# A planner's cost model recalibrated, and the stores of first contents held until the chunks of x are loaded

## The chip, the cores and the metric

One core of one Trainium2 chip. The metric is device time in microseconds (us) of one launch. The kernel before takes 1199.34 us, the median of 3 runs (1198.03 to 1200.96).

## The reference

Three layers follow one another on 2304 tokens (4 sequences of 576) of width 512.

```python
# attention with decay, 4 x 8 heads, 576 tokens, 64 wide
scores = q @ k.T / 8 + cum[:, None] - cum[None, :]      # cum: running sum of log f; causal
x = softmax(scores) @ v                                 # -> [2304, 512]
# dense MLP
h = x @ w_in                                            # [2304, 2048]
x = (h * sigmoid(1.702 * h)) @ w_out                    # [2304, 512]
# 8 experts, the best 2 for each token, noisy gate
logits = x @ w_gate + log1p(exp(x @ w_noise)) * noise
out[t] = sum over the 2 experts e: weight * (relu(x[t] @ w1[e]) @ w2[e])
```

## The kernel before, in words

**Precision.** Each operand of a product is split into a rounded part (`h`, hi) and the rest (`l`, lo), and a product is three matmuls: hi·hi, hi·lo, lo·hi. The rounding is done by `rounded` (lines 327 to 335), the rest by `subtract` (lines 337 and following). Both offer several ways: the rounding on VectorE (DVE, L333), ScalarE (ACT, L334) or GpSimd (POOL, L335), the subtraction on VectorE (L338) or GpSimd (L339). Both read and write SBUF alone.

**Stages.** The *attention* runs over 16 pairs of heads, four to a sequence (batch): loads of q, k and v, splits, scores (L600 to L666), maximum (DVE), exponential (ACT L589), transposes (L727), product with v (L773), store of the result to `x2` in DRAM (L781). The *dense MLP* runs over 9 chunks of 256 tokens and four quarters Q of its hidden width; a chunk in a quarter is 48 matmuls of 256 columns (`h`, L982) and 24 of 512 columns (`y`, L1002), with a gelu between (`gelu`, L957 to L961: tanh on ACT, a product on DVE, the split gh and gl). `xprep` (L920 and following) brings a chunk of x: four loads of 256 KB (L933: `xa` and a second summand into the tile that later is the hi part), two loads of the softmax's reciprocals (L938, into the later lo part), an addition and a multiplication (L927 on DVE or L928 on POOL), the rounding on ACT (L948) and the subtraction. Chunks 0 to 5 (`early_c`) do quarter 0 as *fillers* between the attention's products; their results go to DRAM (`yp`, L1050) and are read back later (`yload`, L1128, into `yacc`). The last two of them stay in SBUF (`kept`); chunks 0 to 3 (`back`) are loaded a second time. After the attention, quarter 0 runs over chunks 6, 7 and 8 (`rest`), and quarters 1 to 3 over kept, rest, back. The last quarter goes with *routing*: each chunk's rows are scattered into a table `tab` in DRAM (L1282). The *experts* then read the table, 640 slots each, and add their rows to `out` by scattering DMAs (L1524). Before that the table and `out` must hold their first contents: `prefill` stores 40 blocks of 258 KB to `tab` (L1076) and 23 blocks of 256 KB of zeros to `out` (L1079), all from one SBUF tile `padr`. It begins when the attention's end is planned (`a_done`) and has the lowest rank among that stage's transfers, 10200.

**The order of the work.** Nothing is ordered by hand. `Planner` runs every part as a thread of a modelled core while the program is built, and the instructions are written out in the order of the modelled start times; each engine then executes its queue in that order, so an instruction that waits holds up all behind it on its engine. A thread yields (engine, us, emit) or several such ways; the way that the model can start first is taken, and among those that can start at about the same time the lowest rank. Costs come from small formulas: `mm` for matmuls, `act`, `dve`, `pool1`, `pool2` for the vector engines, `dma` for transfers. A transfer holds SP's queue for 0.475 us, lands by the running total `moved`, and none is begun while `moved` is more than 2.1 us ahead (`DEEP`).

```python
self.moved = max(self.moved, t + 1.1) + us                 # run(): a transfer of `us`
us = max(self.moved, t + 0.475 * (starts - 1) + 1.1 + us / starts) - t
def mm(n, count=1):  return count * (max(n, MMN) / 2400 + 0.0025)      # MMN = 128
def dma(nbytes):     return 0.05 + nbytes / 360e3
yield ("DMA", 2.9, load, 4)                                # xprep: 1 MB of a chunk
yield ("go", one_op(("DMA", 1.46, rload, 2), rok))         # xprep: 512 KB of reciprocals
```

Of the kernel before, what the change touches and what calls it, by code (L numbers as in the profile page):

```python
# [35 lines left out]
class Tokens:  # L36
    """Numbered buffers that threads take and give back."""
# [17 lines left out]
class Planner:  # L55
    """Runs generators as threads of a modelled core and emits their instructions in the order of
    the modelled start times, so that every engine's queue holds what can start first.

    A thread yields (engine, us, emit), a Tokens (it is sent the number taken), (Tokens, number) to give
    one back, an Event to wait for, ("set", Event), or ("go", generator, priority)."""  # L60
# [5 lines left out]
    SLACK = 0.05  # L66

# [73 lines left out]
    def run(self, until=None):  # L141
        while until is None or until.at is None:
            best = None
            for e, q in self.ready.items():
                if not q:
                    continue
                free = max(self.busy[e], self.moved - self.DEEP) if e == "DMA" else self.busy[e]
                t0 = min(max(x[4], free) for x in q)
                pick = min((x for x in q if max(x[4], free) <= t0 + self.SLACK), key=lambda x: x[:2])
                t = max(pick[4], free)  # L150
                if best is None or t < best[0]:
                    best = (t, e, pick)
            if best is None:
                assert until is None, "threads wait for one another"
                return
            t, e, pick = best
            _, _, th, (us, emit, *starts), _, entries = pick
            for e2, x in entries:
                self.ready[e2].remove(x)
            self.now = max(self.now, t)  # L160
            emit()
            if e == "DMA":
                starts = starts[0] if starts else 1
                self.busy[e] = t + 0.475 * starts
                self.moved = max(self.moved, t + 1.1) + us
                us = max(self.moved, t + 0.475 * (starts - 1) + 1.1 + us / starts) - t
            else:
                self.busy[e] = t + us
            th.at = t + us + self.LAT[e]
            th.last = e  # L170
            self.step(th, None)
# [26 lines left out]
def mm(n, count=1):  # L198
    return count * (max(n, MMN) / 2400 + 0.0025)


def dma(nbytes):
    return 0.05 + nbytes / 360e3


TR = 0.109


@with_exitstack
def tile_attn_mlp_moe(ctx, tc, q, k, v, f, w_in, w_out, gates, noise, w1, w2, out):  # L210
    """q: [pair, (head d), (tokens 512.., 0..511)], k: [head, d, token], v: [pair, p, i, head, d] of the tokens 128 i + p
    (the last 64: any tokens), w_in and w1: [.., block, p, k, n] of the rows 128 k + p and columns 128 block + n,
    gates: [p, k, (gate, noise)], noise: [p, t, e] of the tokens 128 t + p; w_in and w_out: 64-bit words."""
# [83 lines left out]
    # ------------------------------------------------------------------ weights  # L297
# [17 lines left out]
    class Weight:  # L315
        """A [128, 512] block of weights, split, for `uses` users."""
# [10 lines left out]
    def rounded(dst, src, n, scale=1.0, kind=""):  # L327
        """dst = scale * src, rounded to dst's type."""
        w = onec if scale == 1.0 else eighth
        at = src.base_partition()  # L330
        w = w[at:at + src.shape[0]]
        ones = bass.AP(tensor=w.tensor, offset=w.offset, ap=[list(w.ap[0])] + [[0, x] for x in src.shape[1:]])
        return ways(kind, ("DVE", dve(n / 2), lambda: nc.vector.tensor_scalar(dst, src, scale, None, op0=OP.mult)),  # L333
                ("ACT", act(n, True), lambda: nc.scalar.activation(dst, src, AF.Copy, scale=scale)),  # L334
                ("POOL", pool1(n), lambda: nc.gpsimd.tensor_tensor(dst, src, ones, op=OP.mult)))  # L335

    def subtract(dst, a, b, n, kind=""):
        return ways(kind, ("DVE", dve(n), lambda: nc.vector.tensor_tensor(dst, a, b, op=OP.subtract)),  # L338
                ("POOL", pool2(n), lambda: nc.gpsimd.tensor_tensor(dst, a, b, op=OP.subtract)))  # L339

    def wprep(src, wt, pool, letter):
        """A DRAM block of [128, 512] -> a rounded part and the rest; `wd`: of 64-bit words."""
# [14 lines left out]
        if wd:  # L357
            pair = raw.bitcast(F32).rearrange("p (n w) -> p n w", w=2)
            low = raw.bitcast(U32).rearrange("p (n w) -> p n w", w=2)[:, :, 0]
            top, val = pair[:, :, 1], pair[:, :, 0]  # L360
            ut = yield utok
            g = stg.tile([128, n], F32, name="wg_", tag=f"wg{ut}")
            u = stg.tile([128, n], U32, name="wu_", tag=f"wu{ut}")
            gi = g.bitcast(U32)
            yield ("ACT", act(n, True), lambda: nc.scalar.activation(g, top, AF.Abs))
            yield ("DVE", dve(n / 2), lambda: nc.vector.tensor_scalar(g, g, TINY, None, op0=OP.max))
            yield ("DVE", dve(n / 2), lambda: nc.vector.tensor_scalar(
                u, gi, 3, 0x3FFFFFFF, op0=OP.logical_shift_left, op1=OP.bitwise_and))
            yield ("DVE", dve(n), lambda: nc.vector.scalar_tensor_tensor(
                u, top.bitcast(U32), 0xC0000000, u, op0=OP.bitwise_and, op1=OP.bitwise_or))  # L370
            yield ("DVE", dve(n), lambda: nc.vector.scalar_tensor_tensor(
                low, low, 29, u, op0=OP.logical_shift_right, op1=OP.bitwise_or))
            yield (utok, ut)
            sl = yield pool
            yield (pre, ahead)
# [12 lines left out]
    # ------------------------------------------------------------------ attention  # L388
# [5 lines left out]
    def attention(actx):  # L394
# [52 lines left out]
        def pair(p):  # L447
# [3 lines left out]
            # loads  # L451
# [46 lines left out]
            def qside(h, end):  # L498
# [6 lines left out]
                if p < QBD:  # L505
                    op = rounded(hb, src, S, sc)
                else:
                    op = ("DMA", 0.41, lambda: nc.sync.dma_start(hb.bitcast(F32), hi.bitcast(F32)))
# [57 lines left out]
            # score tiles  # L566
# [5 lines left out]
            def tile_(i):  # L572
# [113 lines left out]
                # transposed probabilities  # L686
# [63 lines left out]
            def pv(h, g):  # L750
# [28 lines left out]
                if g == 1:  # L779
                    hh = hp * 2 + h  # L780
                    yield ("DMA", 0.9, lambda: nc.sync.dma_start(  # L781
                        x2[hh, :, :, b * S:(b + 1) * S].rearrange("a d t -> (a d) t"), t))
# [43 lines left out]
    # ------------------------------------------------------------------ set-up  # L826
# [70 lines left out]
    # ------------------------------------------------------------------ dense MLP  # L897
# [22 lines left out]
    def xprep(c, x):  # L920
# [5 lines left out]
        def both(op, z):  # L926
            return ways("xa", ("DVE", dve(n), lambda: nc.vector.tensor_tensor(xa, xa, z, op=op)),  # L927
# [92 lines left out]
    # chunks that the first batches fill run between the attention's products  # L1020
# [4 lines left out]
    def filler(c, prio, before, read):  # L1025
# [21 lines left out]
        def out_():  # L1047
            for z in both:
                yield z
            yield ("DMA", 1.46, lambda: nc.sync.dma_start(  # L1050
# [19 lines left out]

    def prefill():
        yield pad_ok
        yield a_done
# [52 lines left out]
    def yload(c):  # L1126
        yield ypd[c]
        yield ("DMA", 1.46, lambda: nc.sync.dma_start(  # L1128
            yacc[:, 2 * c:2 * c + 2], yp[c * CH:(c + 1) * CH].rearrange("(t p) d -> p t d", p=128)))
        yield ("set", yin[c])  # L1130

# [232 lines left out]
    # ------------------------------------------------------------------ experts  # L1364
# [22 lines left out]
    def group(gi_):  # L1387
# [56 lines left out]
        # products  # L1444
# [52 lines left out]
    def second(gi_, H_, hev, ids, wab, prio, xet):  # L1497
# [44 lines left out]
        # the last of the parts go block by block, so that the last group's blocks end one after another  # L1542
# [44 lines left out]
    # ------------------------------------------------------------------ rows past an expert's slots  # L1587
# [54 lines left out]
def lay(I):  # L1642
    """The arrays as the kernel takes them; no element changes."""
# [43 lines left out]
```

## Time and profile before

| what | us |
|---|---|
| median of the runs (3) | 1199.34 |
| the profiled execution: its span, first to last instruction | 1201.4 |
| TensorE (PE) busy | 1128.1 |
| VectorE (DVE) busy | 751.1 |
| ScalarE (ACT) busy | 529.2 |
| GpSimd (POOL) busy | 299.4 |

The time of the profiled execution is given by its span; nothing that lies around it is listed apart. Its span is 2.1 us above the median of the runs. "Busy" of PE counts a matmul from its start to its modelled end, so overlapping matmuls and waits between two that overlap can hide in it; the number of matmuls in a stretch tells more. PEclk is the granted share of TensorE's clock. SPq is the queue of SyncE, from which all transfers but the scattering ones are issued.

### The profile page before, as it was taken

To read this page: it belongs to the slowest core of one execution; us is meant where nothing else is said; L and a number is where in the kernel's file an instruction comes from. 1 tells how busy PE (TensorE), PEld (TensorE's weight loads), DVE (VectorE), ACT (ScalarE), POOL (GpSimd) and SP (SyncE) were. 2 spreads that over 40 slices of the span, in tenths; PEclk is the share of its full clock that TensorE was granted. 3 is DMA by queue.
4 is the path that set the end of the run, shared out by engine and by line. 5 is a ranking of instruction groups with operands and counts; after the bars stand their busy time and mean duration, and the time that the engine had idled before them with its cause. 6 is when DMAs were issued, how large, how long until landed. Compare 5 with 4: busy or idle time off the path is not lost.

```text
span 1201.4 us, 18895 instructions
## 1 busy us (share of the span) xinstructions
PE 1128.1 (94%) x6905; PEld 1000.0 (83%) x6905; DVE 751.1 (63%) x1609; ACT 529.2 (44%) x1251; POOL 299.4 (25%) x316
## 2 busy tenths in 40 slices
PE   7998999999897999999999988999999999999993
PEld 6777888887796998998988877889998989899993
DVE  8999999975558747745777875645434343434410
ACT  4687777674353424433333343544333333333311
POOL 4457654410214001000132343112020202020202
PEclk7998899999898999999999988999999999999997
DMA  8668657619999903101021357676363636262503
GB/s 217 185 189 225 167 153 184 171 66 235 278 280 263 361 2 97 44 1 37 15 96 75 117 160 223 189 191 181 83 152 83 153 78 152 77 158 71 115 1 46
DMA packets 92096, 167.46 MB, mean 139 GB/s; under 512 B 9310, under 2 KB 29534, under 8 KB 91994
## 3 DMA queue, kind: packets, MB, share of 16 engines
q1 hardware_dynamic: 83354, 146.17, 43.1%
q0 software_dynamic: 8640, 20.00, 7.9%
q8 instruction: 56, 0.92, 0.3%
q14 instruction: 46, 0.38, 0.1%
HBM read 112.60 MB, written 49.40 MB: 135 GB/s over the span
## 4 chain that ended last, share of the span: by engine, by line
PE 61%; DVE 15%; DMA 12%; issue 5%; ACT 3%; POOL 2%; SPq 1%; another core or an unknown queue 0%; POOLq 0%; DVEq 0%; ACTq 0%
PE h L1483 15%; PE ye L1540 14%; PE y L1002 12%; PE h L982 12%; PE PT L727 2%; PE O L773 2%; DMA out<-yt,ids 2%; DVE kb L338 1%; DMA xl<-rd 1%; DVE qa L338 1%; DMA xh<-x 1%; POOL out L1524 1%; DVE pt24l L445 1%; DMA xrh<-x 1%; DVE m L585 1%
## 5 line engine op out<-in xcount | busy, mean ns | idle before, releaser
L1467 DVE SCALAR_TENSOR_TENSOR hl<-h,hh 128x320 fp32r<-128x320 f32 (+1 forms) x112 | 56.1, 501 | 213.4 <-ACT hh L1466 212.1
L1466 ACT ACTIVATE hh<-h 128x320 fp32r<-128x320 f32 (+1 forms) x112 | 50.0, 446 | 232.2 <-PE h L1483 232.1
L1524 POOL DMA_INDIRECT out<-yt,ids x36 | 58.5, 1625 | 348.6 <-ACT yt L1519 341.1
L1002 PE MATMUL y<-wbh,gh 128*128 128x512 f32 x288 | 117.6, 408 | 9.2 <-POOL gh L961 4.6
L1002 PE MATMUL y<-wbh,gl 128*128 128x512 f32 x288 | 116.1, 403 | 4.5 <-DVE gl L338 2.7
L957 ACT ACTIVATE t<-h 128x256 f32<-128x256 f32 x144 | 55.4, 385 | 139.1 <-PE h L982 119.8
L1540 PE MATMUL ye<-wbh,hh 128*128 128x512 f32 x288 | 114.4, 397 | 1.3 <-ACT hh L1466 1.3
L1002 PE MATMUL y<-wbl,gh 128*128 128x512 f32 x288 | 115.0, 399 | 0.0
L1540 PE MATMUL ye<-wbh,hl 128*128 128x512 f32 x288 | 113.4, 394 | 0.1
L1540 PE MATMUL ye<-wbl,hh 128*128 128x512 f32 x288 | 113.1, 393 | 0.0
L1483 PE MATMUL h<-xtl,wah 128*128 128x320 f32 (+1 forms) x448 | 86.5, 313 | 0.0
L1483 PE MATMUL h<-xth,wah 128*128 128x320 f32 (+1 forms) x448 | 86.0, 313 | 0.0
L1483 PE MATMUL h<-xth,wal 128*128 128x320 f32 (+1 forms) x448 | 85.7, 313 | 0.0
L589 ACT ACTIVATE e<-S,m 128x384 f32<-128x384 f32 (+3 forms) x128 | 67.3, 530 | 37.2 <-DVE m L585 19.1
L958 DVE SCALAR_TENSOR_TENSOR t<-t,h 128x256 f32<-128x256 f32 x144 | 59.5, 417 | 29.1 <-ACT t L957 26.7
L1483 PEld LDWEIGHTS h<-xth,wah 128*128 128x128 f32 x448 | 73.1, 188 | 4.0
L382 ACT CAST wbh<-wraw 128x512 fp32r<-128x512 f32 x96 | 59.8, 626 | 33.3 <-DMA wraw<-in_w 16.2
L960 ACT CAST gh<-t 128x256 fp32r<-128x256 f32 x126 | 51.0, 407 | 53.1 <-DVE t L958 52.4
L1002 PEld LDWEIGHTS y<-wbh,gl 128*128 128x128 f32 x288 | 55.1, 191 | 21.2 <-DVE gl L338 5.0
L1483 PEld LDWEIGHTS h<-xtl,wah 128*128 128x128 f32 x448 | 72.1, 188 | 0.4
L1483 PEld LDWEIGHTS h<-xth,wal 128*128 128x128 f32 x448 | 71.7, 187 | 0.0
L1002 PEld LDWEIGHTS y<-wbh,gh 128*128 128x128 f32 x288 | 54.9, 191 | 20.1 <-POOL gh L961 5.2
(421 smaller groups left out, 2782.8 us busy)
## 6 DMA issues: line engine op xcount, KB each, us to landing
wraw<-in_w SPq DMA_DIRECT2D x160, 256.0 KB
tab<-padr SPq DMA_DIRECT2D x40, 258.0 KB
rk<-in_k SPq DMA_DIRECT2D x32, 288.0 KB
x<-xo SPq DMA_DIRECT2D x32, 288.0 KB
wraw<-in_w_in SPq DMA_DIRECT2D x16, 512.0 KB
wraw<-in_w_out SPq DMA_DIRECT2D x16, 512.0 KB
xe<-tab SPq DMA_DIRECT2D x6, 1290.0 KB
xa<-x SPq DMA_DIRECT2D x26, 256.0 KB
```

Of the source, the lines that this page charges most:

```text
L382: yield ("ACT", act(n, True), lambda: nc.scalar.copy(hi, val))
L589: yield ("ACT", act(n, extra=2), lambda: nc.scalar.activation(ev[:, h], o, AF.Exp, bias=m[:, h:h + 1], scale=1.0, accum_out=sa[:, 8 * hp + ...
L957: yield ("ACT", act(CH), lambda: nc.scalar.activation(t, h, AF.Tanh, scale=0.851))
L958: yield ("DVE", dve(CH), lambda: nc.vector.scalar_tensor_tensor(t, t, 1.0, h, op0=OP.add, op1=OP.mult))
L960: yield ways("gh", ("ACT", act(CH, True), lambda: nc.scalar.copy(gh, t)), ("POOL", pool1(CH), lambda: nc.gpsimd.tensor_tensor(gh, t, onec. ...
L982: nc.tensor.matmul(h, a[:, kk], z[:, kk], start=(i == 0), stop=(i == len(ops) - 1))
L1002: nc.tensor.matmul(y, a[:, t * 128:(t + 1) * 128], b, start=(fl == 0 and n == 0), stop=(fl == FPQ - 1 and n == 2))
L1466: yield ("ACT", act(c1 - c0), lambda: nc.scalar.activation(hh[:, c0:c1], ps, AF.Relu))
L1467: yield ("DVE", dve(c1 - c0), lambda: stt(hl[:, c0:c1], ps, 0.0, hh[:, c0:c1].bitcast(F32), op0=OP.max, op1=OP.subtract))
L1483: nc.tensor.matmul(ps, a[:, kk], z[:, kk, c0:c1], start=(i == 0), stop=(i == len(ops) - 1))
L1524: st = nc.gpsimd.indirect_dma_start(out=out, out_offset=bass.IndirectOffsetOnAxis(ap=ids[:, b:b + 1], axis=0), in_=yt, in_offset=None, com ...
L1540: nc.tensor.matmul(ye[b][0], a[:, b * 128:(b + 1) * 128], w, start=(j == 0 and n == 0), stop=(j == FB - 1 and n == 2))
```

## The change

Four groups of edits, and docstrings and comments that go.

```diff
@@ class Planner
+    SHARED = 1.8
@@ Planner.run
-                self.moved = max(self.moved, t + 1.1) + us
-                us = max(self.moved, t + 0.475 * (starts - 1) + 1.1 + us / starts) - t
+                self.moved = max(self.moved, t + 1.7) + us
+                us = max(self.moved, t + 0.475 * (starts - 1) + 1.7 + us / starts) - t
             else:
+                if e == "DVE" and starts and self.busy["POOL"] > t:
+                    us *= self.SHARED
                 self.busy[e] = t + us
@@ costs
 def mm(n, count=1):
-    return count * (max(n, MMN) / 2400 + 0.0025)
+    return count * max(0.109, 0.0024 + n * 0.0004506)
 def dma(nbytes):
-    return 0.05 + nbytes / 360e3
+    return 0.05 + nbytes / RATE
+RATE = 240e3
@@ rounded, subtract, wprep's four DVE steps, xprep's add and multiply: the DVE way gets a mark
-        return ways(kind, ("DVE", dve(n / 2), lambda: ...),
+        return ways(kind, ("DVE", dve(n / 2), lambda: ..., "sbuf"),
@@ attention: q, k, v loads, qb copy, x2 store; filler's yp store, yload
-            yield ("go", one_op(("DMA", 0.82, lambda: nc.sync.dma_start(RQ, q[p])), qe))
-            yield ("go", one_op(("DMA", 1.64, ldk, 2), ke))
-            yield ("go", one_op(("DMA", 0.91, lambda: nc.sync.dma_start(vt, v[p])), ve))
+            yield ("go", one_op(("DMA", dma(128 * S * 4), lambda: nc.sync.dma_start(RQ, q[p])), qe))
+            yield ("go", one_op(("DMA", dma(256 * S * 4), ldk, 2), ke))
+            yield ("go", one_op(("DMA", dma(128 * 640 * 4), lambda: nc.sync.dma_start(vt, v[p])), ve))
...
@@ xprep
-        yield ("DMA", 2.9, load, 4)
-        yield ("wait", -3.0)
-        yield ("go", one_op(("DMA", 1.46, rload, 2), rok))
-        yield ("wait", 3.0)
+        yield ("DMA", 6.3, load, 4)
+        yield ("wait", -6.4)
+        yield ("go", one_op(("DMA", 3.1, rload, 2), rok))
+        yield ("wait", 6.4)
@@ prefill
+    fill_go = event()
     def prefill():
         yield pad_ok
-        yield a_done
+        yield fill_go
@@ after yload
+    def filling():
+        for c in early_c:
+            yield yin[c]
+        for c in back:
+            yield xgo[c]
+            yield X[c].ready
+        yield ("set", fill_go)
+    P.go(filling(), base)
```

So the model charges a transfer 1/240000 us a byte in place of 1/360000 and 0.6 us more of latency, a chunk of x 9.4 us in place of 4.36, a matmul of 512 columns 0.233 us in place of 0.216, one of 256 columns 0.118 in place of 0.109, one of 128 columns 0.109 in place of 0.056; a marked VectorE step costs 1.8 times its price if GpSimd is busy when it starts. The cost of one of the 63 stores (0.74 and 0.73) stays. No instruction is added or removed; which engine does a rounding or a subtraction, and the order of every queue, can come out otherwise. The stores become available once the early chunks' partial results are back in SBUF and chunks 0 to 3 of x are loaded and split a second time, in the model's time.

## Rows read from the trace of the kernel before

**Rows 1.** The page, part 1: busy time and share of the span.

```profile
PE 1128.1 (94%) x6905; PEld 1000.0 (83%) x6905; DVE 751.1 (63%) x1609; ACT 529.2 (44%) x1251; POOL 299.4 (25%) x316
```

**Rows 2.** Windows: stretch, length, busy of PE, PEld, DVE, ACT, POOL; PEclk, DMA share, GB/s.

```profile
0.00:280.00 280.00, 256.48 (x1701) 220.78 (x1702) 252.46 (x400) 197.85 (x541) 136.14 (x115) 0.95 0.64 174
285.00:320.00 35.00, 28.48 (x155) 24.04 (x154) 17.01 (x22) 11.00 (x23) 8.45 (x8) 0.87 1.10 254
320.00:358.00 38.00, 38.00 (x235) 33.84 (x235) 22.84 (x44) 19.17 (x41) 4.49 (x3) 0.98 1.07 294
358.00:390.00 32.00, 24.84 (x136) 20.26 (x135) 28.93 (x40) 13.06 (x26) 14.38 (x8) 0.89 1.00 260
390.00:420.00 30.00, 30.00 (x198) 27.15 (x197) 22.61 (x46) 12.23 (x28) 2.23 (x2) 1.00 1.03 366
420.00:570.00 150.00, 150.00 (x970) 135.62 (x969) 87.16 (x179) 53.45 (x125) 8.27 (x8) 1.00 0.12 36
690.00:760.00 70.00, 60.02 (x356) 52.16 (x355) 47.04 (x150) 30.16 (x63) 24.15 (x31) 0.88 0.64 193
```

**Rows 3.** The chain that ended last, in order of time: start, length, what.

```profile
286.26 7.74 DMA xrh<-x
294.01 8.92 DMA xl<-rd
302.95 10.49 DMA yacc<-yp
...
418.02 5.56 PE y L1002 x24
423.58 5.51 PE h L982 x48
```

**Rows 4.** Timeline of SP's queue: start, length, merged instructions.

```profile
303.99 0.36 SPq L1076 DMA_DIRECT2D tab<-padr  x1
...
320.02 2.39 SPq L1076 DMA_DIRECT2D tab<-padr  x4
...
334.32 13.09 SPq L1076 DMA_DIRECT2D tab<-padr  x12
347.62 0.34 SPq L355 DMA_DIRECT2D wraw<-in_w_in  x1
...
398.24 17.35 SPq L1079 DMA_DIRECT2D out<-padr  x23
```

**Rows 5.** Timeline of DVE, 362 to 369 us; in brackets the idle time before.

```profile
362.82 1.23 DVE L927 TENSOR_TENSOR xa<-xa,xh 128x1024 f32<-128x1024 f32 x1 [2.12 <-issue]
363.97 0.41 DVE L958 SCALAR_TENSOR_TENSOR t<-t,h 128x256 f32<-128x256 f32 x1
...
366.11 2.58 DVE L338 TENSOR_TENSOR gl<-t,gh 128x256 fp32r<-128x256 f32 x1
```

**Rows 6.** Timeline of PE, 362 to 370 us.

```profile
364.87 0.50 PE L1002 MATMUL y<-wbh,gh 128*128 128x512 f32 x1 [3.10 <-ACT gh L960]
...
368.74 0.80 PE L1002 MATMUL y<-wbh,gl 128*128 128x512 f32 x1 [1.47 <-DVE gl L338]
```

**Rows 7.** Timeline of POOL, 365 to 369 us.

```profile
365.59 2.82 POOL L928 TENSOR_TENSOR xa<-xa,xl 128x1024 f32<-128x1024 f32 x1
```

**Rows 8.** Line L338 in 0 to 280 us: durations ns min/median/max, first and last start.

```profile
L338 DVE TENSOR_TENSOR kb<-rk,ka x21: 740/1039/2921, 13.7 to 245.6; 64x576 fp32r<-64x576 f32 x21
L338 DVE TENSOR_TENSOR qa<-rq,qa x16: 751/754/2890, 13.0 to 246.9; 64x576 fp32r<-64x576 f32 x16
```

**Rows 9.** Groups by line in 0 to 280 us: busy us, mean ns, idle before.

```profile
L338 DVE TENSOR_TENSOR kb<-rk,ka 64x576 fp32r<-64x576 f32 x21 | 26.2, 1263 | 0.1
L338 DVE TENSOR_TENSOR qa<-rq,qa 64x576 fp32r<-64x576 f32 x16 | 19.3, 1206 | 0.5
```

**Rows 10.** Line L339, the same subtraction on POOL, 0 to 280 us.

```profile
L339 POOL TENSOR_TENSOR qa<-rq,qa x16: 1406/1559/1933, 9.1 to 244.1; 64x576 fp32r<-64x576 f32 x16
```

**Rows 11.** The tile of the table: its scatters.

```profile
L1282 POOL DMA_INDIRECT tab<-pay,si x36: 957/963/1323, 598.3 to 734.8; - x36
```

More of the change, by code (lines that the diff above doesn't have):

```diff
@@ L332, in rounded @@
         ones = bass.AP(tensor=w.tensor, offset=w.offset, ap=[list(w.ap[0])] + [[0, x] for x in src.shape[1:]])
-        return ways(kind, ("DVE", dve(n / 2), lambda: nc.vector.tensor_scalar(dst, src, scale, None, op0=OP.mult)),
+        return ways(kind, ("DVE", dve(n / 2), lambda: nc.vector.tensor_scalar(dst, src, scale, None, op0=OP.mult), "sbuf"),
                 ("ACT", act(n, True), lambda: nc.scalar.activation(dst, src, AF.Copy, scale=scale)),
@@ L337, in subtract @@
     def subtract(dst, a, b, n, kind=""):
-        return ways(kind, ("DVE", dve(n), lambda: nc.vector.tensor_tensor(dst, a, b, op=OP.subtract)),
+        return ways(kind, ("DVE", dve(n), lambda: nc.vector.tensor_tensor(dst, a, b, op=OP.subtract), "sbuf"),
                 ("POOL", pool2(n), lambda: nc.gpsimd.tensor_tensor(dst, a, b, op=OP.subtract)))
@@ L365, in wprep @@
             yield ("ACT", act(n, True), lambda: nc.scalar.activation(g, top, AF.Abs))
-            yield ("DVE", dve(n / 2), lambda: nc.vector.tensor_scalar(g, g, TINY, None, op0=OP.max))
+            yield ("DVE", dve(n / 2), lambda: nc.vector.tensor_scalar(g, g, TINY, None, op0=OP.max), "sbuf")
             yield ("DVE", dve(n / 2), lambda: nc.vector.tensor_scalar(
-                u, gi, 3, 0x3FFFFFFF, op0=OP.logical_shift_left, op1=OP.bitwise_and))
+                u, gi, 3, 0x3FFFFFFF, op0=OP.logical_shift_left, op1=OP.bitwise_and), "sbuf")
             yield ("DVE", dve(n), lambda: nc.vector.scalar_tensor_tensor(
-                u, top.bitcast(U32), 0xC0000000, u, op0=OP.bitwise_and, op1=OP.bitwise_or))
+                u, top.bitcast(U32), 0xC0000000, u, op0=OP.bitwise_and, op1=OP.bitwise_or), "sbuf")
             yield ("DVE", dve(n), lambda: nc.vector.scalar_tensor_tensor(
-                low, low, 29, u, op0=OP.logical_shift_right, op1=OP.bitwise_or))
+                low, low, 29, u, op0=OP.logical_shift_right, op1=OP.bitwise_or), "sbuf")
             yield (utok, ut)
@@ L507, in qside @@
                 else:
-                    op = ("DMA", 0.41, lambda: nc.sync.dma_start(hb.bitcast(F32), hi.bitcast(F32)))
+                    op = ("DMA", dma(64 * S * 4), lambda: nc.sync.dma_start(hb.bitcast(F32), hi.bitcast(F32)))
                 yield ("go", one_op(op, both))
@@ L780, in pv @@
                     hh = hp * 2 + h
-                    yield ("DMA", 0.9, lambda: nc.sync.dma_start(
+                    yield ("DMA", dma(128 * S * 4), lambda: nc.sync.dma_start(
                         x2[hh, :, :, b * S:(b + 1) * S].rearrange("a d t -> (a d) t"), t))
@@ L926, in both @@
         def both(op, z):
-            return ways("xa", ("DVE", dve(n), lambda: nc.vector.tensor_tensor(xa, xa, z, op=op)),
+            return ways("xa", ("DVE", dve(n), lambda: nc.vector.tensor_tensor(xa, xa, z, op=op), "sbuf"),
                     ("POOL", pool2(n), lambda: nc.gpsimd.tensor_tensor(xa, xa, z, op=op)))
@@ L1049, in out_ @@
                 yield z
-            yield ("DMA", 1.46, lambda: nc.sync.dma_start(
+            yield ("DMA", dma(CH * DM * 4), lambda: nc.sync.dma_start(
                 yp[c * CH:(c + 1) * CH].rearrange("(t p) d -> p t d", p=128), got.ys))
@@ L1127, in yload @@
         yield ypd[c]
-        yield ("DMA", 1.46, lambda: nc.sync.dma_start(
+        yield ("DMA", dma(CH * DM * 4), lambda: nc.sync.dma_start(
             yacc[:, 2 * c:2 * c + 2], yp[c * CH:(c + 1) * CH].rearrange("(t p) d -> p t d", p=128)))
         yield ("set", yin[c])
+    def filling():
[5 more added lines that the diff above has]
+        yield ("set", fill_go)
     for i, c in enumerate(rest):
```

## The prediction, made before the changed kernel was run

> **What bounds the kernel now.** I read four views in this order: the page's busy shares, windows by stage, the chain that ended last, and the timelines of the queues where PE stood still.
>
> PE is busy 94% [rows 1], so at first sight little can be gained. That number hides waits; the count of matmuls in a stretch doesn't. Where PE runs without a wait, one chunk of the dense MLP is 24 matmuls of 512 columns in 5.56 us and 48 of 256 in 5.51 us [rows 3]: 72 in 11.07 us, or 0.154 us each. By this measure 390 to 420 us is full (198 x 0.154 = 30.4 of 30 us) and 420 to 570 us as well [rows 2]. The stretches just before are not: 155 matmuls in 35 us are 23.8 us of work, 235 in 38 us are 36.1, 136 in 32 us are 20.9. Between 285 and 390 us PE loses 11.2 + 1.9 + 11.1 = **24.2 us**, and there the granted clock falls to 0.87 and 0.89 of full speed as well [rows 2]: a mean between PE's levels of 1.2 and 2.4 GHz, after stretches in which PE stood idle. The 16 DMA engines are at 1.00 to 1.10 of a full share throughout, moving 254 to 294 GB/s [rows 2].
>
> Two kinds of work make up that DMA load. From 285 to 320 us it is the chunks of x and the read-back of partial results: the chain goes through xrh, xl and yacc at 7.7 to 10.5 us each [rows 3]. Up to 320 us a single first-content store is among them; then they come in numbers, and SP needs 13.09 us to issue 12 of them, with the next weight load behind on the same queue [rows 4].
>
> How a late transfer reaches PE is seen at 361 us. DVE's addition for a chunk of x starts at 362.82 after 2.12 us of idling; the gelu product, which needs nothing of x, stands behind it in the queue [rows 5], and PE has waited 3.10 us for the gh that follows from it [rows 6]. Right after, POOL works on xa from 365.59 to 368.41 [rows 7], DVE's small gl subtraction takes 2.58 us in that time [rows 5], and PE waits another 1.47 us for it [rows 6]. So two errors of the old cost model (transfers too fast, DVE undisturbed by POOL) put instructions into the queues in a bad order, and both are what the change prices.
>
> The attention, 0 to 280 us, is another bound: DVE is busy 252 of 280 us, ACT 198, POOL 136 [rows 2]. Part of DVE's time is crowding. The 64x576 subtraction takes 0.74 to 0.75 us at best, 1.26 and 1.21 us on average, 2.9 us at worst [rows 8, 9]: 21 x (1.263 - 0.740) + 16 x (1.206 - 0.751) = 18.3 us over 37 instructions.
>
> **The change part by part.**
>
> *The stores held back.* 63 stores, 40 x 258 KB and 23 x 256 KB, 16.6 MB, leave the stretch before the second loading of x ends and go behind it. The three issues shown are 17 stores from 304 to 348 us [rows 4], 4.4 MB; at the 254 to 294 GB/s of these stretches [rows 2] they take 15 to 17 us of DMA time, and up to 13 us of SP's queue at one go [rows 4]. Without them the loads of x behind end some 15 us earlier, and PE, which stands in 358 to 390 us for what hangs on them, loses less. Of those 11.1 us I take back 9: the two stalls of rows 6 alone, with PE's slow clock after them, make up most of it, and the second has another cause than a transfer. Bounds: 0 (the loads of x set the pace themselves) and 11.1.
>
> *Where the stores go.* Behind the last chunk's load, from about 360 us on, 16.6 MB at the 366 GB/s that 390 to 420 us shows [rows 2] take 45 us, that is to about 410 or, if they start late, 450. The cover is an idle DMA: share 0.12 from 420 to 570 us [rows 2]. Who needs them: the first scatter into the table at 598.3 [rows 11], 150 us later. On SP, weight loads stand behind a store's issue; 23 stores took 17.35 us [rows 4] in a stretch in which PE lost nothing, so I cost it at 0. If the cover were gone (a quarter's weights falling into those 45 us), it would be one load's wait, 1 to 3 us.
>
> *The slower transfers in the model* (240 against 360 GB/s, 0.6 us more latency, 9.4 us for a chunk of x against 4.36). The measured pieces of a chunk, 7.7 to 10.5 us on the chain [rows 3], say that the new price is near the truth when DMA is full. Expected: additions for x are queued later on DVE and POOL, and the read-back of partial results (10.49 us on the chain [rows 3], ranked behind the rest chunks) no longer slips in front. That acts on the 11.2 us of 285 to 320 us. But the loads of the rest chunks can't begin before the attention's last results are stored, so I take back 4, with bounds 0 and 8.
>
> *The matmul prices* 0.233 and 0.118 us agree with 5.56/24 = 0.232 and 5.51/48 = 0.115 [rows 3]; by themselves 0.
>
> *The crowded DVE.* No instruction is saved; some roundings and subtractions go from DVE to ACT and POOL, others to a time when POOL is idle. A subtraction moved relieves DVE of 0.75 us at the least and costs POOL 1.56 [rows 8, 10], during which other subtractions on DVE are slow. Of the 18.3 us of crowding I take 3, with DVE the bound there. Bounds: a gain of 12 (two thirds of it) and a loss of 11 (below).
>
> The Trainium skill, SBUF — State Buffer, section "Who interferes with whom", speaks against the form of this price: whichever of the two starts first holds the shared port for its whole instruction and the other is blocked, it is not slowed by a factor. Rows 5 and 7 agree: gl ends 0.28 us after POOL's xa. Under that rule a factor of 1.8 leaves the planner surprised by a stall such as the second of rows 6, and the sum would be 1.5 us less gain.
>
> *Routing and experts* (690 us on): nothing priced anew acts strongly there; 690 to 760 us loses time and has a clock of 0.88 [rows 2], and a reshuffled order may move it either way. 0, bounds -4 and +4.
>
> **Sum.** -9 - 4 - 3 = -16 us on the profiled execution's span of 1201.4, so 1185.4; that execution lies 2.1 us above the median 1199.3, so **1183 us** as a median.
>
> **The rivals.**
>
> *More of it (1168 us).* The attention also balances: crowding falls by 12 and the stretch 285 to 390 regains 19: 1199 - 31. For it: POOL is busy only 136 of 280 us and ACT 198 [rows 2]. Against it: every POOL instruction added crowds DVE again. The Trainium skill, Perfetto Trace Analysis, "Optimizing Scalar/DVE Operations", says that offloading between those two might not help because they share a port; the averages of rows 9 bear it out, and the chance is kept low.
>
> *The loads of x set the pace anyway (1197 us).* Up to 320 us, where only one store had been issued [rows 4], DMA was already full and PE lost as much as later [rows 2]. If the seven chunks' own bytes decide, the stalls stay, and 2 us are left of the gain.
>
> *Slower: a filler slips past the attention's end (1207 us).* At 286 us the loads for the last filler chunk are only coming in [rows 3], so one and a bit of six fillers is still to do. The new model charges a filler's load twice as much, its matmuls 8% more and its DVE steps up to 1.8 times, while fillers rank last. If the plan puts one more behind the attention and the attention gets no shorter, PE has 11.07 us more to do there; with 3 us regained in the stalls, 1199 + 8 = 1207. It decides as soon as two whole fillers are left at the end of the last v product. Against it: PE's idle time in the attention stays, and work can fill it.
>
> **How the numbers follow.** Forecast (1173 to 1192 about 1183) 0.42; more of it 0.18; loads set the pace 0.15; slower 0.25. A measurement here can tell about 0.2%, 2.4 us, from no change. Faster: 0.42 + 0.18 + 0.06 of the third case = 0.66. Same: the 0.09 left of it. Slower: 0.25. Range 1166 to 1208: it leaves out about half of the case "more of it" (0.08) and four tenths of the slower one (0.10). Its lower end is the forecast less the unspent bounds of the stretch and a part of the attention's; the upper is one filler. The forecast's own range is 1173 to 1192.
>
> **What would show it.** Right: all 63 stores begin after the last load of a chunk of x; the stretch between the attention's end and some 400 us holds as many matmuls as 390 to 420 us did; no PE wait over 2 us on gh there. The mean of the 64x576 subtraction on DVE falls below 1.2 us. Wrong: the attention's last v product comes later than 280 us, the end of the attention's stretch now, or two whole filler chunks follow it; or PE still waits in that stretch while no store is in flight, which would make the x loads the bound; or weight loads stand behind stores on SP while PE waits.

## The result, and the profile after

The changed kernel takes 1207.12 us, the median of 4 runs (1204.77 to 1208.75); the kernel before, on the same chip, 1198.68 us (4 runs, 1197.72 to 1200.96). The ratio is 1.0053, 95% interval 1.0027 to 1.0079: **slower by half a per cent** (the two medians alone stand 0.7% apart), where 1183 and "faster" were forecast. The profiled execution took 1206.77 us with a span of 1204.9, so 1.87 us lie around the span. The two profiled spans differ by 3.5 us, less than the 8.4 us of the medians: the execution of before whose rows are shown was a long one. The other 4.9 us can't be seen in these two traces.

The page's busy row of the changed kernel (busy us, share of the span, instructions):

```profile
PE 1125.2 (93%) x6905; PEld 997.9 (83%) x6905; DVE 745.8 (62%) x1588; ACT 525.8 (44%) x1254; POOL 326.2 (27%) x334
```

Against [rows 1], PE and DVE are as before and only POOL has more to do. The windows of the changed kernel, over the stretches of [rows 2] (stretch, us, then busy time and instructions of PE, PEld, DVE, ACT and POOL, PEclk, DMA share, GB/s):

```profile
0.00:280.00 280.00, 254.38 (x1707) 217.15 (x1708) 250.40 (x381) 196.00 (x548) 164.26 (x130) 0.96 0.60 171
285.00:320.00 35.00, 19.63 (x92) 16.50 (x91) 15.66 (x16) 9.10 (x15) 4.66 (x4) 0.74 0.98 209
320.00:358.00 38.00, 38.00 (x245) 34.67 (x244) 22.53 (x42) 17.45 (x40) 4.49 (x5) 0.97 0.65 182
358.00:390.00 32.00, 29.03 (x169) 25.23 (x168) 25.77 (x40) 13.49 (x29) 9.94 (x8) 0.95 0.87 197
390.00:420.00 30.00, 30.00 (x203) 27.32 (x202) 23.73 (x42) 13.72 (x28) 9.30 (x9) 1.00 0.76 244
690.00:760.00 70.00, 59.27 (x368) 51.45 (x367) 49.70 (x147) 30.98 (x65) 19.74 (x27) 0.95 0.61 188
```

By the prediction's measure of 0.154 us for a matmul, 358 to 390 us holds 33 matmuls more than before (169 against 136), which is 5.1 us regained, in the place that was named; 320 to 358 us is now full. But 285 to 320 us holds 92 where it held 155: 63 x 0.154 = **9.7 us newly lost**, with the clock down at 0.74 of full speed.

What PE waited for there, in the timeline of PE (start, us; in brackets the idle time before and what ended it):

```profile
292.01 1.22 PE L986 MATMUL h<-xrh,wah 128*128 128x256 f32 x4 [5.61 <-ACT xrh L952]
...
304.74 0.50 PE L1006 MATMUL y<-wbh,gl 128*128 128x512 f32 x1 [1.01 <-POOL gl L343]
...
316.71 1.22 PE L986 MATMUL h<-xrh,wah 128*128 128x256 f32 x4 [8.66 <-ACT xrh L952]
```

Two waits of 5.61 and 8.66 us for the rounded chunk of x (`xrh`) of the last two fillers. The kernel before has none: its longest wait for a chunk of x in the fillers is 0.53 us, for `xrl`. The chain that ended last, followed back from the second one, says why for that one (start, us, what):

```profile
304.74 3.32 PE y L1006 x13
308.06 0.02 issue
308.08 0.61 ACT ys L1047
308.70 0.37 SPq L1054
309.07 0.04 issue
309.11 0.58 SPq L942
309.69 0.04 issue
309.74 4.50 DMA xrl<-rd
...
314.35 1.24 DVE xa L931
315.59 0.02 issue
315.61 1.05 ACT xrh L952
```

The load of the reciprocals, `xrl<-rd` (L942), which the last filler's x needs, begins only when the store of the *previous* filler's result (L1054) has been issued, and that store waits for PE's last y and the copy on ACT. PE waits for x, and x waits for PE. SP's own queue shows the order (timeline of SP):

```profile
297.70 0.57 SPq L937 DMA_DIRECT2D xa<-x  x1
298.71 0.57 SPq L937 DMA_DIRECT2D xrh<-x  x1
299.35 0.60 SPq L937 DMA_DIRECT2D xa<-x  x1
299.99 0.61 SPq L937 DMA_DIRECT2D xrh<-x  x1
308.70 0.37 SPq L1054 DMA_DIRECT2D yp<-ys  x1
309.11 1.38 SPq L942 DMA_DIRECT2D xrl<-rd  x2
```

The four loads of x are issued by 300.6 us, the two of the reciprocals at 309.11: in between SP stood 8.0 us on the store, by its waits from 282 to 312 us:

```profile
SPq L1054 <- ACT ys L1047: 13.9, 2, 8.0
```

The loads of the filler before it, whose wait is the first, stand behind stores as well: SP waited 8.1 us for DVE before it stored the reciprocals at 272.00 us (L439), and stored a filler's and the attention's results before it came to x. The kernel before issues these loads ahead of the reciprocals and of the attention's results, 6.8 us earlier (SP's timelines; first the changed kernel, then the kernel before):

```profile
277.87 0.64 SPq L937 DMA_DIRECT2D xa<-x  x1
```

```profile
271.08 0.62 SPq L933 DMA_DIRECT2D xa<-x  x1
```

The loss doesn't last. The dense MLP ends at 692.4 us (before 692.1), and the group of the experts' products that ends at 794.7 us before ends at 794.0, both read from PE's timelines. What is left of the span's 3.5 us arises behind that: PE's 4701st matmul of 6905 still starts 0.7 us earlier than before, its 4801st 3.8 us later. Between them PE waits for the experts' table rows, 4.66 us instead of the 1.00 us of the same step before (timelines of PE; first the changed kernel, then the kernel before):

```profile
807.14 4.07 PE L1441 MATMUL tr<-identf,xe 128*128 128x128 f32 x20 [4.66 <-DMA xe<-tab]
```

```profile
807.95 2.40 PE L1426 MATMUL tr<-identf,xe 128*128 128x128 f32 x20 [1.00 <-DMA xe<-tab]
```

Such small differences between two single traces say little. The kernel before and the one with the stores alone held back (first experiment below) have the same order on PE up to the 2006th matmul, and yet the attention's last v product comes at 279.2 us in the one trace and at 281.9 in the other.

The crowding on DVE is where it was (groups by line and form: busy us, mean ns, idle before):

```profile
L342 DVE TENSOR_TENSOR kb<-rk,ka 64x576 fp32r<-64x576 f32 x15 | 20.8, 1389 | 0.0
L342 DVE TENSOR_TENSOR qa<-rq,qa 64x576 fp32r<-64x576 f32 x14 | 18.9, 1350 | 0.4
```

Against the best durations after, 737 and 752 ns, that is 15 x 0.652 + 14 x 0.598 = 18.2 us on 29 instructions, where [rows 8, 9] gave 18.3 us on 37. Eight subtractions went away and the mean of those that stayed rose. Why, the timelines of DVE and POOL show (changed kernel; a slow one and the POOL operation beside it, then a quick one):

```profile
78.51 1.87 DVE L342 TENSOR_TENSOR qa<-rq,qa 64x576 fp32r<-64x576 f32 x1
77.86 1.90 POOL L343 TENSOR_TENSOR qa<-rq,qa 64x576 fp32r<-64x576 f32 x1
```

```profile
92.44 0.75 DVE L342 TENSOR_TENSOR qa<-rq,qa 64x576 fp32r<-64x576 f32 x1
92.49 1.97 POOL L343 TENSOR_TENSOR qa<-rq,qa 64x576 fp32r<-64x576 f32 x1 [0.40 <-DVE qa L337]
```

Of the 66 subtractions in the two traces up to 280 us, every one that starts inside a POOL tensor operation (more than 0.05 us behind its start, with more than 0.1 us to go) ends 0.61 or 0.62 us after that operation, as the first does here. The others take 0.74 to 0.755 us, even where POOL starts just behind them, as in the second. Caught in this way were 20 of 37 before and 21 of 29 after; the undisturbed ones fell from 17 to 8. So DVE was relieved of the quick ones.

### The profile page after: what moved, and what is told of

Same layout as the page of the kernel before. It is cut to its first block, busy times and chain, and to the rows that moved or that the text cites. A ratio compares the mean times of both kernels' runs of the same rounds, so it can differ in the third digit from the quotient of the medians.

```text
span 1204.9 us, 18879 instructions
## 1 busy us (share of the span) xinstructions
PE 1125.2 (93%) x6905; PEld 997.9 (83%) x6905; DVE 745.8 (62%) x1588; ACT 525.8 (44%) x1254; POOL 326.2 (27%) x334
## 4 chain that ended last, share of the span: by engine, by line
PE 71%; DVE 13%; issue 5%; DMA 3%; ACT 3%; POOL 3%; SPq 1%; POOLq 0%; ACTq 0%; DVEq 0%
PE h L1498 16%; PE ye L1555 15%; PE h L986 15%; PE y L1006 15%; PE O L777 3%; PE PT L731 2%; PE tr L1441 1%; DMA xrl<-rd 1%; DVE pt24l L449 1%; DMA xe<-tab 1%; DVE m L589 1%; ACT e L593 1%; DMA out<-yt,eids 1%; DVE qa L342 1%; DVE kb L342 1%
## 5 line engine op out<-in xcount | busy, mean ns | idle before, releaser
L965 POOL TENSOR_TENSOR gh<-t,onec 128x256 fp32r<-128x256 f32 x21 | 16.0, 764 | 247.6 <-DVE t L962 223.0
L593 ACT ACTIVATE e<-S,m 128x128 f32<-128x128 f32 (+3 forms) x128 | 67.8, 536 | 30.3 <-DVE m L589 16.3
L731 PE MATMUL PT<-identf,e 128*128 128x128 f32 (+1 forms) x400 | 64.6, 287 | 13.0 <-ACT e L593 9.0
```

The lines of the kernel that those rows point to most:

```text
L593: yield ("ACT", act(n, extra=2), lambda: nc.scalar.activation(ev[:, h], o, AF.Exp, bias=m[:, h:h + 1], scale=1.0, accum_out=sa[:, 8 * hp + ...
L731: nc.tensor.transpose(ps[0:w.shape[1], o:o + 128], w, identf)
```

## The experiments

Each kernel is the changed file with parts set back or altered, so line numbers are those of after; all compute the same function. Each was timed in five rounds beside the kernel before, whose median in the five series was 1198.3 to 1199.7 us. The expectations name the theories by letters. After the result stood, in the main, these: that the slower transfer prices make the new waits for x (A); that one other part alone makes them (B) or the lost time (C, of the matmul prices); that no part does it, because any shift of a price writes another order (D); and that the split of a chunk's loads into two steps of 6.3 and 3.1 us lets the store in between (E).

**Each part alone** (the kernel before with one part of the change).

Stores held back, old prices:

```diff
 def prefill():
-        yield a_done
+        yield fill_go
```

> Only the later begin of the 63 stores; all prices as before. If the stores stood in the way of the loads of x (the prediction's first term), PE's waits in 358 to 390 us fall and the time falls by 5 to 9 us against before (1190 to 1194). If the loads set the pace themselves, within 2.4 us of before. The attention and the loads up to 300 us must stand as before in either case.

1204.44 us, ratio 1.0035 (1.0017 to 1.0053). Windows of this kernel, and SP's waits from 320 to 360 us (total, times, longest):

```profile
320.00:358.00 38.00, 34.24 (x183) 29.10 (x182) 21.72 (x37) 15.33 (x32) 5.35 (x4) 0.87 0.60 155
358.00:390.00 32.00, 28.04 (x169) 24.30 (x167) 25.71 (x40) 14.89 (x31) 10.04 (x6) 0.95 0.85 209
```

```profile
SPq L937 <- DVE xl L342: 11.6, 1, 11.6
```

and what ends that wait (timelines of DVE and of SP):

```profile
352.40 1.23 DVE L342 TENSOR_TENSOR xl<-xa,xh 128x1024 fp32r<-128x1024 f32 x1 [0.15 <-ACT xh L952]
353.66 0.57 SPq L937 DMA_DIRECT2D xa<-x  x1
```

This is worse than either reading in the expectation allowed. With the stores out of the way the DMA is only 0.60 busy from 320 to 358 us, and PE does 183 matmuls there, not 235 [rows 2]. The loads of x don't begin earlier: for 11.6 us they stand on a buffer, the raw tile `xa`, which comes free when DVE's subtraction has read an earlier chunk out of it. That chunk, loaded from 332 us on, was itself ready only then. So the stores had filled a DMA that isn't full without them.

Transfer prices alone:

```diff
-    self.moved = max(self.moved, t + 1.1) + us
+    self.moved = max(self.moved, t + 1.7) + us
 # and the other lines of the change that price a transfer: RATE, dma(), 6.3 and 3.1
```

> Only the transfer prices (240 GB/s, 0.6 us more latency, 9.4 us for a chunk of x). Theory A, that these prices put the last fillers' loads of x too late on SP's queue, behind a store that waits for PE: two PE waits on xrh of 5 us or more between the attention's end and 320 us, as in the changed kernel (6.0 and 9.1), and a time 5 to 10 us above before. Theory B, that the crowded-VectorE price or the matmul prices moved those loads: no such waits, time within 4 us of before.

1193.85 us, ratio 0.9945 (0.9925 to 0.9965): faster than either theory expected, and without the waits of A. Its window from 360 to 420 us, and that of before:

```profile
360.00:420.00 60.00, 58.72 (x376) 52.45 (x375) 50.07 (x91) 24.69 (x56) 4.19 (x4) 1.00 0.83 240
```

```profile
360.00:420.00 60.00, 52.84 (x314) 45.41 (x313) 49.58 (x81) 23.51 (x52) 16.62 (x10) 0.94 1.01 314
```

62 matmuls more, 9.5 us by the measure of 0.154; its longest wait for `xrh` is 3.91 us.

The crowded price alone:

```diff
+    SHARED = 1.8
+    if e == "DVE" and starts and self.busy["POOL"] > t:
+        us *= self.SHARED
```

> Only the factor of 1.8 on marked VectorE steps while GpSimd is busy. Theory A: no PE wait on xrh over 3 us, the attention ends up to 4 us earlier than before and the time is 0 to 5 us below before. Theory B: the xrh waits are here and the time is 5 to 10 us above before.

1204.40 us, ratio 1.0036 (1.0018 to 1.0054). With the *old* transfer prices it already has the wait (timeline of PE):

```profile
317.50 1.23 PE L986 MATMUL h<-xrh,wah 128*128 128x256 f32 x4 [10.22 <-ACT xrh L952]
```

So the transfer prices aren't needed for it. It isn't the same wait, though: here the last filler's six loads are issued together, from 300.51 to 307.48 us, behind those of two other chunks, and SP hardly waits for a filler's result (0.3 us).

The matmul prices alone:

```diff
-    return count * (max(n, MMN) / 2400 + 0.0025)
+    return count * max(0.109, 0.0024 + n * 0.0004506)
```

> Only the matmul prices (128 columns 0.109 us in place of 0.056, 256 and 512 columns 8% more). Theory A: no PE wait on xrh over 3 us, time within 4 us of before. Theory B: fillers slip behind the attention's end, waits on xrh, time 5 us or more above before.

1226.35 us, ratio 1.0224 (1.0195 to 1.0252). The edit that the prediction costed at nothing is, alone, the worst of the four. It has no wait over 2.32 us for `xrh`; its last v product comes at 290.1 us, against 279.2 before.

**One part left out** (the change with one part set back to the old code).

```diff
 # without the matmul prices
-    return count * max(0.109, 0.0024 + n * 0.0004506)
+    return count * (max(n, MMN) / 2400 + 0.0025)
```

> The change without its matmul prices. Theory C, that the matmul prices are what turned the change's sign (alone they cost 2.2%): the attention ends before 265 us as with the transfer prices alone (258.4) and the time is 1190 to 1197. Theory D, that the parts' effects do not add because each price change reshuffles the whole order: the time lies anywhere from 1190 to 1215, and the attention's end does not follow the matmul price.

1192.18 us, ratio 0.9942 (0.9922 to 0.9962): 15 us below the change and faster than before, though the wait is still there:

```profile
292.01 1.23 PE L986 MATMUL h<-xrh,wah 128*128 128x256 f32 x4 [8.77 <-ACT xrh L952]
```

```diff
 # without the transfer prices: t + 1.1, 360e3, 2.9, 1.46 and the fixed costs of loads again
-RATE = 240e3
+RATE = 360e3
```

> The change without its transfer prices. Theory C: the costs of the other three stay (stores 0.35%, crowded price 0.36%, matmul 2.2% alone): 1215 to 1235, slower than the change itself. Theory D: no ordering with the change can be told; a time under 1207 would speak for it.

1230.02 us, ratio 1.0271 (1.0236 to 1.0306), with a wait of 11.62 us for `xrh`.

```diff
 # without the crowded price
-    SHARED = 1.8
+    SHARED = 1.0
```

> The change without the factor of 1.8. Theory C: the time stays at 1203 to 1212, since the matmul prices are still in it; the waits on xrh stay. Theory D: a move of over 6 us either way, although the factor alone cost 4 us.

1196.54 us, ratio 0.9982 (0.9960 to 1.0004). No wait for x over 1.62 us is left in the fillers; the last one's:

```profile
304.51 0.74 PE L986 MATMUL h<-xrh,wah 128*128 128x256 f32 x4 [1.13 <-ACT xrh L952]
```

```diff
 # without holding the stores
-        yield fill_go
+        yield a_done
```

> The change with the stores beginning at the attention's end as before. The order up to the attention's end is that of the change, so the waits on xrh of 6 and 9 us stay. If holding the stores back costs (alone 4 us): 1202 to 1206. If it is neutral here, because the slower transfer prices hold them back anyway: within 2.4 us of the change (1204 to 1210).

1208.67 us, ratio 1.0087 (1.0060 to 1.0115): near the change's own 1207.1, so the stores' new place is worth little here too. Its 354 matmuls from 360 to 420 us are the change's 356, with the stores in their old place: what was regained there is the prices' doing.

**The split of a chunk's loads, and the halves of the matmul price.** The change with all six loads of a chunk in one step, so that no store can come between x and its reciprocals:

```diff
-        yield ("DMA", 6.3, load, 4)
-        yield ("wait", -6.4)
-        yield ("go", one_op(("DMA", 3.1, rload, 2), rok))
-        yield ("wait", 6.4)
+        yield ("DMA", 9.4, both_loads, 6)    # load(), then rload()
+        yield ("set", rok)
```

> The change, with the six loads of a chunk of x (four of x, two of reciprocals) issued in one step of 9.4 us, so that no store can be planned between them. Theory E, that the long wait on xrh (9.1 us in the change) is the reciprocals' loads standing on SP behind the store of partial results (L1054), which waits for PE: the second xrh wait falls below 4 us and the time to 1196 to 1203. Rival, that the crowded price makes the last filler's loads late by their own rank: a wait of 5 us or more stays and the time stays over 1203.

1208.62 us, ratio 1.0088 (1.0070 to 1.0106); the waits shrink from 5.61 and 8.66 to 3.59 and 6.35 us only:

```profile
317.95 1.22 PE L987 MATMUL h<-xrh,wah 128*128 128x256 f32 x4 [6.35 <-ACT xrh L953]
```

SP's timeline shows what the last filler's loads now stand behind:

```profile
297.72 0.36 SPq L1055 DMA_DIRECT2D yp<-ys  x1
298.13 0.57 SPq L937 DMA_DIRECT2D xa<-x  x1
...
303.27 0.57 SPq L937 DMA_DIRECT2D xrh<-x  x1
...
305.21 1.29 SPq L942 DMA_DIRECT2D xrl<-rd  x2
```

The store is still first, and a chunk needed later (the load at 298.13 us) comes next. The split explains about 4 of 14.3 us of waiting, and none of the time.

The same step, without the matmul prices:

```diff
-    return count * max(0.109, 0.0024 + n * 0.0004506)
+    return count * (max(n, MMN) / 2400 + 0.0025)
 # and the one step of 9.4 us
```

> The change without its matmul prices (1192.2) and with the six loads in one step. Theory E: its xrh wait of 9.2 us falls below 4 and the time to 1183 to 1190. Rival: the wait stays over 5 us and the time stays at 1189 to 1196.

1190.90 us, ratio 0.9951 (0.9931 to 0.9971): the lowest time of all, though not told apart from the 1192.18 with the split loads.

The change with the 8% of the matmul price but not its floor of 0.109 us, and with the floor alone:

```diff
-    return count * max(0.109, 0.0024 + n * 0.0004506)
+    return count * (0.0024 + max(n, MMN) * 0.0004506)          # slope alone
+    return count * max(0.109, max(n, MMN) / 2400 + 0.0025)     # floor alone
```

> The change with only the 8% on long matmuls, 128 columns at 0.060 as good as before. If the 8% is what costs the 15 us (1207.1 against 1192.2): 1203 to 1211. If the floor of 0.109 is: 1189 to 1196.

> The change with only the floor of 0.109 us for short matmuls, 256 and 512 columns priced as before. If the floor is what costs: 1203 to 1211; if the 8%: 1189 to 1196. Theory D (any new price reshuffles the order and the time moves by up to 10 us either way): e11 and e12 do not add up to the 15 us, and both lie between or both on one side.

Slope alone 1197.91 us, ratio 0.9997 (0.9984 to 1.0011); floor alone 1200.21 us, 1.0009 (0.9993 to 1.0025). Over the 1192.18 with neither, the halves cost 6 and 8 us and both together 15: no half carries it. They nearly add up, which speaks for prices that cost something; it could also mean that any shift of a price costs as much.

**A price shifted by half a per cent**, which says nothing about the chip: the matmul price of the change, of the kernel before, and of the transfer prices alone, times 1.005 and times 0.995.

```diff
-    return count * max(0.109, 0.0024 + n * 0.0004506)
+    return 1.005 * count * max(0.109, 0.0024 + n * 0.0004506)   # or 0.995; the change
+    return 1.005 * count * (max(n, MMN) / 2400 + 0.0025)        # or 0.995; the other two
```

> The change with all matmul prices 0.5% higher, which tells the planner nothing new. If the prices order the work worse in a lasting way: 1204 to 1210, as the change. If the order scatters (theory D): the time can lie anywhere from 1192 to 1215, and differs from the change's 1207.1 by over 4 us.

> The change with all matmul prices 0.5% lower. As for 0.5% higher: 1204 to 1210 if the cause is in the prices, a difference of over 4 us from 1207.1 if the order scatters.

> The kernel before with all matmul prices 0.5% higher. If small shifts do not matter: within 2.4 us of before. If the order scatters: a difference of over 4 us, more likely slower, since the order before is one that was good.

> The kernel before with all matmul prices 0.5% lower. Within 2.4 us of before if small shifts do not matter; a difference of over 4 us, more likely slower, if the order scatters.

> Transfer prices alone, matmul prices 0.5% higher. If the gain is lasting: at most 1200, and PE's work from 360 to 420 us at 55 us or more, as in all but one of the kernels with the new transfer prices. If it was luck: over 1203, or as spread as before's 1197 to 1223.

> Transfer prices alone, matmul prices 0.5% lower. As the other: at most 1200 and 55 us or more of PE's work from 360 to 420 us if lasting; over 1203 if luck.

| median, us (ratio to the kernel before, 95%) | x 0.995 | x 1 | x 1.005 |
|---|---|---|---|
| the change | 1195.59 (0.9954 to 0.9993) | 1207.12 (1.0027 to 1.0079) | 1200.24 (0.9997 to 1.0038) |
| the kernel before | 1223.42 (1.0181 to 1.0238) | 1198.68 | 1197.28 (0.9966 to 1.0004) |
| transfer prices alone | 1211.25 (1.0068 to 1.0138) | 1193.85 (0.9925 to 0.9965) | 1202.12 (1.0009 to 1.0049) |

No row rises or falls steadily, and each spans 11.5 us or more: more than the change itself, and as much as any of its parts but the matmul prices. The last two runs were the test of the transfer prices as a gain that lasts; 1200 us or less was wanted from both, and both missed it, though PE's work from 360 to 420 us, 60.00 and 58.46 us, was the 55 or more that was wanted with it. In the changed kernel, 0.5% on a price rewrites PE's order from the 217th (x 0.995) or 220th (x 1.005) of its 6905 matmuls on, at 36 us.

The 2% of the kernel before at x 0.995 shows what a bad draw is made of. PE's longest sums of waits up to 280 us, for that kernel and then for the kernel before (total us, times, longest):

```profile
PE PT L731 <- ACT e L593: 14.0, 9, 3.9
PE S L604 <- DVE qa L342: 5.4, 1, 5.4
```

```profile
PE PT L727 <- ACT e L589: 5.7, 7, 2.0
PE S L600 <- DVE qa L338: 3.8, 1, 3.8
```

The transposes wait longer for the exponentials, and these two make 9.9 us more of waiting; the last v product comes at 289.0 us and not at 279.2. That is 9.8 of this span's 16.9 us. The rest has arisen by 440 us: PE's 2451st matmul starts at 438.7 us and not at 422.0. Its window from 360 to 420 us, with the old transfer prices, and that of the transfer prices alone at x 0.995:

```profile
360.00:420.00 60.00, 53.59 (x316) 45.50 (x315) 50.19 (x78) 27.02 (x56) 14.04 (x9) 0.95 0.98 268
```

```profile
360.00:420.00 60.00, 58.46 (x373) 52.11 (x372) 45.46 (x75) 25.88 (x56) 16.62 (x14) 1.00 0.74 193
```

Both kernels lose against the kernel before, but only the first loses here.

**Over all 20 kernels.** Matmuls from 360 to 420 us: 354 to 382 in 12 of the 13 with the new transfer prices (326 in the one with the floor alone), 310 to 338 in all 7 with the old. Some 45 matmuls, 6 to 8 us, are gained there with the transfer prices whatever the rest of the order does. It isn't that PE only comes there late: the transfer prices alone lose nothing from 285 to 320 us (166 matmuls) and gain, the crowded price alone loses there (82) and doesn't. A wait of 6 us or more for a chunk of x in the fillers: 9 of the 11 kernels with the crowded price, 2 of the 4 with new transfer prices and no crowded price, none of the 5 with both old. Neither price is needed by itself, and both open the door. In eight of the eleven kernels that have such a wait, all with the new transfer prices and split loads, SP's timeline has a filler's store directly ahead of the reciprocals' loads; in the other three, the two with the crowded price and old transfer prices and the one with the loads in one step, the filler's loads stand together behind other chunks'.

Most of the scatter has arisen by 440 us: PE's 2451st matmul starts between 407.9 and 442.2 us in these kernels, and its last one follows it (correlation 0.93 over the 20).

*One part, in several orders.* Where two of these kernels differ in one part alone, the medians differ so: the matmul prices +27.7, +14.9 and +17.7 us (added to the kernel before, to the change without them, to the one step without them), the crowded price +5.7 and +10.6, the stores +5.8 and -1.6, the transfer prices -4.8, +4.8, -12.2 and -22.9. The matmul prices cost in all three. That they make a lasting worse order, beside the scatter, is a rival that these runs leave standing; against it stands that the change with the same prices shifted by 0.5% takes 6.9 and 11.5 us less.

## Why the prediction was wrong, point by point

*The stores, -9 us: 0 or a little worse.* The work named (loads of x behind stores) was in the timeline, but what released those loads was a buffer that an earlier chunk held, not the stores' end: the prediction's own lower bound, "the loads of x set the pace themselves", is what the run of the stores alone shows, and its wait of 11.6 us names the buffer. A full DMA share was taken for a cause; the row to read was what SP's load waits for. One of the prediction's signs of being wrong came too: in the changed kernel PE waits 5.61 and 8.66 us up to 316.71 us, while the first of the 63 stores is issued at 392.65.

*Where the stores go, 0: right.* 390 to 420 us stays full, 203 matmuls, with the stores in it.

*Slower transfers, -4: mis-sized, and in the other place.* They were to act from 285 to 320 us, where the changed kernel lost 9.7 us; they act from 358 on and are worth 6 to 8 us of PE's work there, part of which the prediction had booked under the stores. Rows 5 and 6 were read rightly: the additions for late chunks are queued later, and PE's waits there shrink.

*Matmul prices, 0: failed as a way of costing.* They agree better with the chip, and alone the time rises by 2.2%. "By themselves 0" asks what a price is worth in its stretch. A price has no place: it shifts every start time behind it and so the whole written order.

*Crowded DVE, -3: 0.* 18.2 us against 18.3. The Trainium skill's rule that the prediction weighed (SBUF — State Buffer, "Who interferes with whom") holds that one of the two engines keeps the port for a whole instruction. The traces agree with it and not with a factor: all 41 caught subtractions end 0.61 or 0.62 us after the POOL operation in which they start, and take 0.77 to 2.92 us by what was left of it. With POOL busy 164 and not 136 us up to 280 us, 21 of 29 were caught and not 20 of 37. So the price had the wrong form, and relieved DVE in the main of subtractions that had cost nothing extra.

*Routing and experts, 0 within 4: right in size.* One wait is longer by 3.66 us; what makes it was not tested.

**The step that failed** is the sum: it adds local effects as though the rest of the order stood still, and allows "a reshuffled order" its plus or minus 4 us in the routing alone. The parts measured alone come to +5.8, -4.8, +5.7 and +27.7 us, 34.3 together; the change that joins them measures +8.4. And three versions of one kernel, 0.5% apart in a price without meaning anything, spread over 11.5 to 26 us. So this change's sign can't be told from one draw of that scatter: with 0.5% on one price the same change is faster than before (0.9974, interval 0.9954 to 0.9993), and the kernel before is 2% slower than itself.

*The rival at 1207 us* met the time by luck, and it is by the same luck that 1207 lies inside the range, whose upper end was this rival's one filler. It was to decide when two whole fillers are left at the last v product. Two and a bit were left already in the kernel before: its last three fillers end at 289.1, 305.3 and 323.9 us, its last v product at 279.2; the prediction counted "one and a bit". After, they end at 286.4, 308.0 and 331.8 us, with the v product at 276.4. The fillers left are three in both; they waited for their x, and the time lost there was made good by 692 us.

*Settled and open.* Shown: the stores bring nothing; the transfer prices regain 6 to 8 us of PE's work at 360 to 420 us; the changed kernel's waits for x come from loads that stand behind stores; the parts don't add up; scatter as large as the change. Open: where the 8.4 us between the medians arise, of which these traces show 3.5; and whether the new prices, those of the matmuls above all, give a better or a worse order on average. The means of three are 1201.0 us for the change, 1206.5 for the kernel before and 1202.4 for the transfer prices, and three draws this wide can't tell. Four versions beat both kernels beyond their intervals, 1190.90, 1192.18, 1193.85 and 1195.59 us; nothing shows that they are more than good draws.

## What to carry to other kernels

Where a planner writes the order, time an edit of its prices at several neighbouring values before crediting it, and credit only what holds in its own stretch at all of them. Before booking a gain for clearing a busy resource, read what releases the transfer that you want earlier: here a buffer did, and the stores had cost nothing. On a queue that runs in order, look for a store that waits for an engine's results ahead of a load which that engine needs.

## What was not expected of the hardware

The crowding of DVE by POOL kept its sum, 18.2 against 18.3 us, while eight of 37 instructions left; it is no slowing but a wait, to within 0.01 us the same 0.61 us from the end of POOL's operation in 41 of 41 cases, so that what a subtraction costs hangs on when it starts. One and the same program, the kernel before, gave single runs from 1193.25 to 1204.57 us in one series of 29 (0.9%), so that a few runs and one profiled execution don't place it to half a per cent; its first three runs had given 1198.03 to 1200.96.
